# Token-block sums of a two-layer kernel: smaller column-tiled matmuls in place of a fold step, and a planner that expects later loads

## The chip, the cores and the metric

The kernel runs on one core of a Trainium2 chip. A core has a matrix engine (TensorE; PE in the profile, with its weight loads shown as PEld), a vector engine (VectorE, DVE), a scalar engine (ScalarE, ACT), a general engine (GpSimd, POOL), and a synchronising engine (SyncE, SP) that here only issues transfers. They share an on-chip memory of 128 partitions (SBUF) and an accumulator memory (PSUM) of eight banks, which TensorE writes. The metric is the device time of one execution in microseconds, as the median of several runs.

## The reference

The inputs are q, k, v of shape 8 x 8 x 576 x 64 (batch, head, token, dimension), a gain `g_norm` of 64, weights `w_in` (512 x 1024) and `w_out` (1024 x 512), and a gain `g_ln` of 1024.

```python
kv  = einsum('bhsd,bhse->bhde', k, v)          # 64 x 64 per head
out = einsum('bhsd,bhde->bhse', q, kv)
x   = out / sqrt(mean(out*out, -1) + 1e-6) * g_norm     # per head, then heads side by side: 4608 x 512
h   = x @ w_in
e   = exp(h - max(h));  solu = h * e / (sum(e) + 1e-9)  # along the 1024
ln  = (solu - mean(solu)) / sqrt(var(solu) + 1e-6) * g_ln
y   = ln @ w_out                                # 4608 x 512, float32
```

## The kernel before

The 4608 tokens are cut into nine chunks of 512: chunk c below 8 holds the first 512 tokens of batch c, and chunk 8 holds the last 64 tokens of all eight batches. The work of a chunk runs through these stages, each a planned piece with a name:

- Loads on GpSimd's queue bring k, v and q of a batch in bfloat16 (`load_kv`, `load_q`, L219 and L228). Batches 0 and 1 are loaded in two halves of four heads, later ones whole. `q_last` (L236) brings the last 64 tokens of a batch for chunk 8.
- `kv_mm` (L286) makes the 64 x 64 products of four head pairs with 64*64 tiles of TensorE; `kv_copy` (L305) copies them to SBUF.
- q is turned so that the head dimension lies along partitions: for chunks 0 to 3 with TensorE (`qT_mm`, L319, and a copy, L327), for chunks 4 to 8 (`XBAR`, L124) with a transposing transfer on SyncE's queue (`q_turn`, L336).
- `o_mm` (L343) multiplies by kv. A square (`sq`), a matmul with a table of means (`s_mm`, L373), a logarithm and an exponential on ScalarE (`ln`, `ex`) and a product on VectorE (`x_mul`, L392) give x, in four quarters (hf, z) per chunk.
- `h_mm` (L471) makes h transposed, 128 of the 1024 features at a time, in eight pieces of four 128x512 matmuls. ScalarE takes the exponential e (L482), VectorE the product u = h*e (L489), GpSimd or ScalarE the square of u (L500, L498), and GpSimd adds e of two pieces (L506).
- The statistics of the last layer are sums over 1024 features for each token: of u, of u*u and of e. `sums` (L531) forms them with TensorE. Its weight `stat_sel` is 32 columns wide, and column i holds 1/1024, so that the sum lands in row i of a quarter of 32 partitions. There are 8 + 8 + 4 = 20 matmuls of 128x512. Matmul n goes to quarter n % 4, so that four work at once, and each quarter ends with a part of each sum. `sums_turn` (L543) transposes 32 x 32 blocks on VectorE from PSUM to SBUF (128x512). `stats_mm` (L549) is the fold step: four float32 matmuls with `fold`, four identity matrices one above another, add up the four parts and put token r of a 128-token block on partition r. `stats` (L559) combines them in four short VectorE operations, and `rstd` (L570) takes the inverse root on ScalarE.
- `out_mm` (L591) multiplies u by the centred `w_out` in halves of four matmuls, two halves for each block of 128 tokens (m = 0 to 3). `scale` (L600) multiplies by rstd into `ob_sb`, and `store` (L607) sends it off on SyncE's queue.

The order of instructions on every engine is fixed before the run by a list scheduler, `Plan.order` (L33). It holds a clock for each engine. It repeatedly takes, among pieces whose needs are planned, the one that can start earliest by its clock, and of equals the one of the lowest rank (L47, L57). A piece can start when its engine is free, when its needs are done, and when the buffers that it claims (`first`) were let go by all their users (`uses`). The length given in `plan.add` is the time that it is believed to take. Loads pass through one shared queue (L75 to L78):

```python
            if load:
                queue = max(queue, t + length + 1.0) + load
                done[n] = queue + 1.3
```

A SyncE transpose counts as done 2.5 after its length (L74). At run time only real semaphores hold an engine up, but each engine executes in the planned order, so whatever waits holds up all behind it. Buffers that matter here: PSUM tags h, out and o have two banks each, s and misc one each. For chunk 0 the sums use a bank of h, for others misc. GpSimd issues the loads, and its own squares and additions stand in the same order.

Of the kernel before, what the change touches and what calls it, by code (L numbers as in the profile page):

```python
# [8 lines left out]
FP32 = mybir.dt.float32  # L9
# [3 lines left out]
MUL = mybir.AluOpType.mult  # L13
SUB = mybir.AluOpType.subtract
AF = mybir.ActivationFunctionType
PSUM = bass.MemoryType.PSUM


class Plan:
# [13 lines left out]
    def order(self):  # L33
        free, done, queue, lanes, mode = {}, {}, 2.5, [], {}
        held = {tag: [] for tag in self.bufs}
        waiting = {n: set(p[4]) for n, p in self.pieces.items()}
        behind = {}
        for n, needs in waiting.items():
            for m in needs:
                behind.setdefault(m, []).append(n)  # L40
        ready = [n for n, needs in waiting.items() if not needs]
        order = []
        while ready:
            best = None
            for n in ready:
                engine, length, rank, fn, needs, first, load = self.pieces[n]
                t = max([free.get(engine, 0.0)] + [done[m] for m in needs])  # L47
                more = {}
                for key in first:
                    old = held[key[0]] + more.setdefault(key[0], [])  # L50
                    more[key[0]].append(key)
                    if len(old) >= self.bufs[key[0]]:
                        last = self.users[old[-self.bufs[key[0]]]]
                        t = max([t] + [done.get(m, 1e9) for m in last])
                if load and len(lanes) >= 8:
                    t = max(t, lanes[-8])
                if t < 1e8 and (best is None or (t, rank) < best[:2]):  # L57
                    best = (t, rank, n)
            t, rank, n = best
            engine, length, rank, fn, needs, first, load = self.pieces[n]  # L60
            ready.remove(n)
            for key in first:
                held[key[0]].append(key)
            if engine == "pe":

                tiling = n[0] if n[0] in ("kv_mm", "o_mm", "sums", "st_mm") else "full"
                length += 0.1 if mode.get(engine, tiling) != tiling else 0.0
                mode[engine] = tiling
            if n[0] == "qT" and engine == "sp":

                if queue > t + 1.0:
                    length, queue = 2.2 * length, queue + 2.0
            free[engine] = t + length
            done[n] = t + length + {"pe": 0.2, "sp": 2.5}.get(engine, 0.12)  # L74
            if load:  # L75
                queue = max(queue, t + length + 1.0) + load
                done[n] = queue + 1.3
                lanes.append(done[n])  # L78
            order.append(fn)
            for m in behind.get(n, ()):  # L80
                waiting[m].discard(n)
                if not waiting[m]:
                    ready.append(m)
        assert len(order) == len(self.pieces)
        return order
# [3 lines left out]
def kernel(  # L89
# [20 lines left out]
    nc = tc.nc  # L110
# [9 lines left out]
    big = ctx.enter_context(tc.tile_pool(name="big", bufs=1))  # L120
# [3 lines left out]
    XBAR = tuple(range(4, NC))  # L124
    bufs = {
        "k": 3, "v": 3, "q": 3, "qT": 3, "osq": 4, "lss": 2, "rst": 2, "oc": 2, "x": 2, "e": 4, "u": 2, "usq": 2, "es": 2,
        "sumT": 2, "ob": 4,
    }

    def bank(key, shape, dtype):  # L130
        return ps.tile(shape, dtype, name=key[0] + "_ps", tag=key[0], bufs=banks[key[0]])

    def tile_of(key, shape, dtype):
        return sb.tile(shape, dtype, name=key[0] + "_sb", tag=key[0], bufs=bufs[key[0]])

    COPIED = ((0, 0),)
    plan = Plan({**banks, **bufs})
    T = {}
# [15 lines left out]

    ident = big.tile([128, 128], BF16, name="ident")
    eye = big.tile([NF, NF], FP32, name="eye")
    fold = big.tile([128, 32], FP32, name="fold")
    zeros = big.tile([128, 512], BF16, name="zeros")
    nc.vector.memset(zeros, 0.0)
    eps_t = big.tile([128, 1], FP32, name="eps_t")  # L160
# [46 lines left out]
        make_identity(nc, ident)  # L207
        make_identity(nc, eye)

    def make_fold():  # L210

        for j in range(4):
            nc.vector.tensor_copy(fold[32 * j:32 * j + 32, :], ident[32 * j:32 * j + 32, 32 * j:32 * j + 32])

    plan.add("ident", "pool", 1.0, -1.95, make_ident)
    plan.add("fold", "dve", 1.0, 0.2, make_fold, ["ident"])


    def load_kv(name, src, b, hs):  # L219
# [310 lines left out]

    def sums(c, part):  # L531
        if part == 0:
            T["sum", c] = bank(("misc" if c else "h", "sum", c), [128, 512], FP32)
        i, src = ((1, T["u", c]), (0, T["usq", c]), (2, T["es", c]))[part]
        n_src = NF // 2 if part == 2 else NF
        for n in range(n_src):
            j = n % 4
            nc.tensor.matmul(  # L538
                T["sum", c][32 * j:32 * j + 32, :], stat_sel[:, i, :], src[:, n, :],
                start=(part == 0 and n < 4), stop=(part == 2), tile_position=(0, 32 * j), skip_group_check=True,  # L540
            )

    def sums_turn(c):  # L543


        t = T["sumT", c] = tile_of(("sumT", c), [128, 4, 4, 32], FP32)
        nc.vector.transpose(t.rearrange("p a b c -> p (a b c)"), T["sum", c][:, :])

    def stats_mm(c):  # L549
        t = T["st", c] = bank(("misc", "st", c), [128, 4, 3], FP32)  # L550
        for g in range(4):
            nc.tensor.matmul(
                t[32 * g:32 * g + 32, :, :], fold[:, :], T["sumT", c][:, :, g, 0:3],
                start=True, stop=True, tile_position=(0, 32 * g),
            )

    small = ctx.enter_context(tc.tile_pool(name="small", bufs=2))

    def stats(c):  # L559

        st = T["st", c]
        w = small.tile([128, 4, 3], FP32, name="w")
        nc.vector.tensor_tensor(out=w[:, :, 1:3], in0=st[:, :, 1:3], in1=factors[:, :, :], op=MUL)
        nc.vector.memset(w[:, :, 0:1], 1.0)
        terms = small.tile([128, 4, 3], FP32, name="terms")
        nc.vector.tensor_tensor(out=terms[:, :, :], in0=st[:, :, :], in1=w[:, :, :], op=MUL)
        T["vare", c] = small.tile([128, 4], FP32, name="vare")
        nc.vector.tensor_reduce(out=T["vare", c][:, :], in_=terms[:, :, :], op=ADD, axis=mybir.AxisListType.X)  # L568

# [50 lines left out]
    for c in range(NC):  # L620
        r, rs = (c + 1, c + 1) if c else (0.55, -0.5)
        parts = [[("u", c, f) for f in range(NF)], [("usq", c, f) for f in range(NF)], [("es", c, n) for n in range(NF // 2)]]
        plan.add(("sums", c), "pe", 1.2, rs + 0.1, lambda c=c: [sums(c, part) for part in range(3)], sum(parts, []),
                 uses=[("u", c), ("usq", c), ("es", c)], first=[("misc" if c else "h", "sum", c)])
        plan.add(("turn", c), "dve", 0.62, rs + 0.14, lambda c=c: sums_turn(c), [("sums", c)],
                 uses=[("misc" if c else "h", "sum", c)], first=[("sumT", c)])
        plan.add(("st_mm", c), "pe", 0.15, rs + 0.15, lambda c=c: stats_mm(c), ["fold", ("turn", c)],
                 uses=[("sumT", c)], first=[("misc", "st", c)])
        plan.add(("stats", c), "dve", 0.65, rs + 0.16, lambda c=c: stats(c), [("st_mm", c)], uses=[("misc", "st", c)])
        plan.add(("rstd", c), "act", 0.45, rs + 0.17, lambda c=c: rstd(c), [("stats", c)])  # L630
        for m in range(4):
            tag = "o" if c == NC - 1 and m > 1 else "out"
            for half in range(2):
                plan.add(("out", c, m, half), "pe", 0.87, r + (2 * m + half) / 8 + 0.01,
                         lambda c=c, m=m, half=half, tag=tag: out_mm(c, m, half, tag),
                         [("w_center", f) for f in range(4 * half, 4 * half + 4)]
                         + [("u", c, f) for f in range(4 * half, 4 * half + 4)] + ([("out", c, m, 0)] if half else []),
                         uses=[("u", c)] + ([(tag, c, m)] if half else []), first=[] if half else [(tag, c, m)])
            plan.add(("ob", c, m), "act" if c == NC - 1 and m % 2 else "dve", 0.67, r + (2 * m + 2) / 8, lambda c=c, m=m: scale(c, m),
                     [("out", c, m, 1), ("rstd", c)], uses=[(tag, c, m)], first=[("ob", c, m)])  # L640
            plan.add(("store", c, m), "act" if c == NC - 1 and m % 2 else "sp", 0.6, r + (2 * m + 3) / 8, lambda c=c, m=m: store(c, m),
                     [("ob", c, m)], uses=[("ob", c, m)])
# [33 lines left out]
```

The softmax here doesn't subtract the row's maximum and nothing guards it: scores larger than these inputs give would overflow.

## Time and profile before

| what | value |
|---|---|
| median of 13 runs | 198.69 us (197.44 to 204.26) |
| the profiled execution, its own time | 199.1 us |
| its span, first to last instruction | 197.3 us |
| TensorE busy | 183.2 us (93%), 1806 matmuls |
| ScalarE, GpSimd, VectorE busy | 140.4, 129.0, 125.9 us |
| sums, L538: matmuls, mean of one | 180, 379 to 384 ns |
| fold step, L552: matmul records, mean of one | 72, 189 ns |
| transposes of sums, L547 | 9, 710 to 716 ns |
| loads of k, v, q, whole, issue to landing (median) | 12.3, 12.4, 14.2 us |
| transposing transfers | 5, 4.3 to 4.5 us |

A matmul's duration includes its way through the array, and neighbours overlap: four 128x512 matmuls that start one after another take 0.86 us in the chain, not four times 379 ns. So costs on TensorE are read from the starts of neighbours. A group's line names the engine, the operation, output and inputs, shapes, the count, the busy time and the mean. In a timeline, what stands in brackets at the end is the idle time of the engine ahead of this piece and what ended it.

### The profile page before, as it was taken

The page shows a single profiled execution, that of the slowest core. Times are in us where ns is not written, and L with a number is a line of the kernel's source. Part 1 is how long each engine was busy: PE and PEld are TensorE (multiplying, and loading weights), DVE is VectorE, ACT ScalarE, POOL GpSimd, SP SyncE. Part 2 cuts the span into 40 slices and gives each one's busy share as a digit, 9 for nine tenths or more (in the row PEclk, how much of TensorE's full clock was granted, in tenths as well). Part 3 has the DMA queues.
Part 4 walks back from the last instruction along what each step waited for, and adds up shares of the span by engine and source line. Part 5 has one row for each costly group of instructions (what it writes and reads, how often), then busy time and mean ns, then how long its engine had stood idle before and what let it go on. Part 6 is the DMA issues. An engine that isn't in the chain of part 4 may idle for free.

```text
span 197.3 us, 4481 instructions
## 1 busy us (share of the span) xinstructions
PE 183.2 (93%) x1806; PEld 82.8 (42%) x1806; DVE 125.9 (64%) x244; ACT 140.4 (71%) x244; POOL 129.0 (65%) x137
## 2 busy tenths in 40 slices
PE   7887988769999989999999999999999999999990
PEld 2442455325445434334444443443454444344430
DVE  2455587464878596578666948767584667665350
ACT  2038887884977899888889697889789296546421
POOL 7971799600899877887898685579194828845200
PEclk9999999978999999999999999999999999999998
DMA  4999999999995999699699983353112011211206
GB/s 52 190 203 293 326 203 205 202 208 242 207 243 53 196 203 241 137 187 210 134 158 228 203 169 115 116 104 120 53 53 74 35 59 51 106 53 70 94 18 195
DMA packets 35892, 29.65 MB, mean 150 GB/s; under 512 B 11800, under 2 KB 30240, under 8 KB 35872
## 3 DMA queue, kind: packets, MB, share of 16 engines
q0 software_dynamic: 20112, 17.30, 53.9%
q1 hardware_dynamic: 15472, 11.54, 20.9%
q10 hardware_dynamic: 288, 0.52, 0.9%
q8 instruction: 14, 0.23, 0.5%
q14 instruction: 6, 0.05, 0.1%
HBM read 32.51 MB, written 9.44 MB: 213 GB/s over the span
## 4 chain that ended last, share of the span: by engine, by line
PE 74%; DMA 11%; POOL 5%; ACT 4%; DVE 3%; issue 1%; POOLq 0%
PE out_ps L595 29%; PE h_ps L474 26%; DMA q_sb<-in_q_dram 7%; PE misc_ps L538 5%; DMA v_sb<-in_v_dram 3%; PE o_ps L354 3%; PE s_ps L375 3%; PE o_ps L595 2%; PE misc_ps L297 2%; POOL usq_sb L500 2%; DVE u_sb L489 1%; POOL k_sb L223 1%; PE misc_ps L198 1%; POOL v_sb L223 1%; PE misc_ps L325 1%
## 5 line engine op out<-in xcount | busy, mean ns | idle before, releaser
L474 PE MATMUL h_ps<-x_sb,w_in_sb 128*128 128x512 bf16 x276 | 70.0, 379 | 1.3 <-DVE x_sb L396 1.1
L595 PE MATMUL out_ps<-w_out_sb,u_sb 128*128 128x512 bf16 x272 | 70.4, 387 | 0.8 <-DVE ob_sb L605 0.7
L500 POOL TENSOR_TENSOR usq_sb<-u_sb 128x512 bf16<-128x512 bf16 x51 | 53.0, 1044 | 24.2 <-DVE u_sb L489 24.1
L506 POOL TENSOR_TENSOR es_sb<-e_sb 128x512 bf16<-128x512 f32 x36 | 45.8, 1274 | 25.7 <-ACT e_sb L482 25.4
L489 DVE TENSOR_TENSOR u_sb<-h_ps,e_sb 128x512 bf16<-128x512 f32 x69 | 47.2, 687 | 23.6 <-ACT e_sb L482 23.1
L482 ACT ACTIVATE e_sb<-h_ps,zero_t 128x512 f32<-128x512 f32 x69 | 47.1, 684 | 11.9 <-PE h_ps L474 11.5
L474 PEld LDWEIGHTS <-w_in_sb 128*128 128x128 bf16 x288 | 27.0, 98 | 34.7 <-issue 4.3
L595 PEld LDWEIGHTS <-u_sb 128*128 128x128 bf16 x288 | 26.9, 99 | 34.6 <-issue 6.6
L605 DVE TENSOR_SCALAR ob_sb<-out_ps,rstd 128x512 f32<-128x512 f32 x33 | 24.6, 746 | 12.0 <-PE out_ps L595 6.5
L396 DVE SCALAR_TENSOR_TENSOR x_sb<-o_ps,g_rep,rst_sb 128x512 bf16<-128x512 f32 x32 | 23.9, 749 | 9.5 <-ACT rst_sb L383 9.4
L369 ACT ACTIVATE osq_sb<-o_ps,zero_t 128x512 bf16<-128x512 f32 x31 | 19.8, 683 | 11.0 <-PE o_ps L354 10.9
L383 ACT ACTIVATE rst_sb<-lss_sb,zero_t 128x512 f32<-128x512 f32 x32 | 23.2, 725 | 0.6
L379 ACT ACTIVATE lss_sb<-s_ps,eps_t 128x512 f32<-128x512 f32 x32 | 22.0, 687 | 0.3 <-PE s_ps L375 0.2
L498 ACT ACTIVATE usq_sb<-u_sb,zero_t 128x512 bf16<-128x512 bf16 x21 | 15.1, 720 | 8.1 <-DVE u_sb L489 7.9
L375 PE MATMUL s_ps<-osq_sb,head_mean 128*128 128x512 bf16 x34 | 13.1, 385 | 0.9 <-ACT osq_sb L369 0.8
L223 POOL DMA_DIRECT2D k_sb<-in_k_dram x10 | 7.9, 788 | 4.1 <-DMA w_in_sb<-in_moe_w_in_dram 2.6
L198 PE MATMUL s_ps<-zeros 128*128 128x512 bf16 x28 | 9.2, 449 | 1.4 <-DVE zero_t L163 1.2
L231 POOL DMA_DIRECT2D q_sb<-in_q_dram x10 | 8.6, 858 | 2.0 <-DMA w_in_sb<-in_moe_w_in_dram 1.6
L315 DVE CAST kvd<-misc_ps 64x128 bf16<-64x128 f32 (+1 forms) x24 | 6.9, 288 | 4.5 <-PE s_ps L297 2.3
L572 ACT ACTIVATE lv<-vare,zero_t 128x4 f32<-128x4 f32 x9 | 2.7, 300 | 9.5 <-DVE vare L568 9.5
L297 PEld LDWEIGHTS <-k_sb 64*64 64x64 bf16 x576 | 6.7, 107 | 4.9 <-issue 4.9
L354 PE MATMUL o_ps<-qT_sb,kvd 64*64 64x32 bf16 (+1 forms) x240 | 8.3, 256 | 0.2 <-ACT qT_sb L332 0.2
(83 smaller groups left out, 139.0 us busy)
## 6 DMA issues: line engine op xcount, KB each, us to landing
out_dram<-ob_sb SPq DMA_DIRECT2D x34, 256.0 KB, 3.4
k_sb<-in_k_dram POOLq DMA_DIRECT2D x6, 576.0 KB, 12.3
v_sb<-in_v_dram POOLq DMA_DIRECT2D x6, 576.0 KB, 12.4
q_sb<-in_q_dram POOLq DMA_DIRECT2D x6, 512.0 KB, 14.2
w_out_f<-in_moe_w_out_dram POOLq DMA_DIRECT2D x1, 2048.0 KB, 16.6
k_sb<-in_k_dram POOLq DMA_DIRECT2D x4, 288.0 KB, 11.6
v_sb<-in_v_dram POOLq DMA_DIRECT2D x4, 288.0 KB, 12.3
q_sb<-in_q_dram POOLq DMA_DIRECT2D x4, 256.0 KB, 12.1
```

Of the source, the lines that this page charges most:

```text
L369: nc.scalar.activation(out=t[:, :], in_=T[("o", *i)].rearrange("p a b c -> p (a b c)"), func=AF.Square, bias=zero_t[:, :])
L375: nc.tensor.matmul(t[:, :], head_mean[:, :], T["osq", i][:, :], start=True, stop=True)
L379: nc.scalar.activation(out=t[:, :], in_=T["s", i][:, :], func=AF.Ln, bias=eps_t[:, :])
L383: nc.scalar.activation(out=t.rearrange("p a b c -> p (a b c)"), in_=T["lss", i][:, :], func=AF.Exp, scale=-0.5, bias=zero_t[:, :])
L396: nc.vector.scalar_tensor_tensor(out=T["x", c][:, 2 * hf:2 * hf + 2, z], in0=T["o", c, hf, z][:, :, :, :], scalar=g_rep[:, :], in1=T["rst" ...
L474: nc.tensor.matmul(t[:, :], w_in_sb[:, dt, f * 128:(f + 1) * 128], T["x", c][:, dt].rearrange("p a b c -> p (a b c)"), start=(dt == 0), st ...
L482: nc.scalar.activation(out=T["e", c, f // 2][:, f % 2, :], in_=T["h", c, f][:, :], func=AF.Exp, bias=zero_t[:, :])
L489: nc.vector.tensor_tensor(out=T["u", c][:, f, :], in0=T["h", c, f][:, :], in1=T["e", c, f // 2][:, f % 2, :], op=MUL)
L500: nc.gpsimd.tensor_tensor(out=dst, in0=src, in1=src, op=MUL)
L506: nc.gpsimd.tensor_tensor(out=T["es", c][:, n, :], in0=e[:, 0, :], in1=e[:, 1, :], op=ADD)
L595: nc.tensor.matmul(T["acc", c, m][:, :], T["u", c][:, f, m * 128:(m + 1) * 128], w_out_sb[:, f, :], start=(f == 0), stop=(f == NF - 1),)
L605: nc.vector.tensor_scalar_mul(out=t[:, :], in0=T["acc", c, m][:, :], scalar1=T["rstd", c][:, m:m + 1])
```

## The change

Two things change. First, in `sums` each matmul of 512 columns becomes four of 128, one to each quarter of 32 partitions. Quarter j takes the tokens of which the place within a block of 128 lies in 32j to 32j + 31, from all four blocks, and adds all sources n itself. No parts are left to be added. The sums fill 128 columns of their bank, VectorE transposes 32 x 32 blocks into the next 128 columns of the same bank, and `stats` reads its three numbers there. The fold matmuls, the fold table and the buffer `sumT` are gone, and the bank of the sums is held until `stats` has read it. The planner's length for the transpose is 0.25 in place of 0.62.

Second, the planner adds `LATE` = 4.0 to the time at which it believes that something has landed: loads of batches 2 and later (k, v, q and `q_last`), and the SyncE transposes. Loads of batches 0 and 1 and of the weights are left as they were.

```diff
+LATE = 4.0
...
-                tiling = n[0] if n[0] in ("kv_mm", "o_mm", "sums", "st_mm") else "full"
+                tiling = n[0] if n[0] in ("kv_mm", "o_mm", "sums") else "full"
...
-            done[n] = t + length + {"pe": 0.2, "sp": 2.5}.get(engine, 0.12)
+            done[n] = t + length + {"pe": 0.2, "sp": 2.5}.get(engine, 0.12) + (LATE if n[0] == "qT" and engine == "sp" else 0.0)
             if load:
                 queue = max(queue, t + length + 1.0) + load
-                done[n] = queue + 1.3
+                done[n] = queue + 1.3 + (0.0 if n[1] in (0, 1) or n == "w_out" else LATE)
...
-            T["sum", c] = bank(("misc" if c else "h", "sum", c), [128, 512], FP32)
+            T["sum", c] = bank(("misc" if c else "h", "sum", c), [128, 2, 128], FP32)
...
         for n in range(n_src):
-            j = n % 4
-            nc.tensor.matmul(
-                T["sum", c][32 * j:32 * j + 32, :], stat_sel[:, i, :], src[:, n, :],
-                start=(part == 0 and n < 4), stop=(part == 2), tile_position=(0, 32 * j), skip_group_check=True,
-            )
+            for j in range(4):
+
+                cols = src[:, n, :].rearrange("p (m j r) -> p j m r", m=4, j=4)[:, j]
+                nc.tensor.matmul(
+                    T["sum", c][32 * j:32 * j + 32, 0, :], stat_sel[:, i, :], cols, start=(part == 0 and n == 0),
+                    stop=(part == 2 and n == n_src - 1), tile_position=(0, 32 * j), skip_group_check=True,
+                )
...
-        t = T["sumT", c] = tile_of(("sumT", c), [128, 4, 4, 32], FP32)
-        nc.vector.transpose(t.rearrange("p a b c -> p (a b c)"), T["sum", c][:, :])
-
-    def stats_mm(c):
-        t = T["st", c] = bank(("misc", "st", c), [128, 4, 3], FP32)
-        for g in range(4):
-            nc.tensor.matmul(
-                t[32 * g:32 * g + 32, :, :], fold[:, :], T["sumT", c][:, :, g, 0:3],
-                start=True, stop=True, tile_position=(0, 32 * g),
-            )
+        T["st", c] = T["sum", c][:, 1, :].rearrange("p (m i) -> p m i", m=4)
+        nc.vector.transpose(T["sum", c][:, 1, :], T["sum", c][:, 0, :])
...
-        plan.add(("turn", c), "dve", 0.62, rs + 0.14, lambda c=c: sums_turn(c), [("sums", c)],
-                 uses=[("misc" if c else "h", "sum", c)], first=[("sumT", c)])
-        plan.add(("st_mm", c), "pe", 0.15, rs + 0.15, lambda c=c: stats_mm(c), ["fold", ("turn", c)],
-                 uses=[("sumT", c)], first=[("misc", "st", c)])
-        plan.add(("stats", c), "dve", 0.65, rs + 0.16, lambda c=c: stats(c), [("st_mm", c)], uses=[("misc", "st", c)])
+        plan.add(("turn", c), "dve", 0.25, rs + 0.14, lambda c=c: sums_turn(c), [("sums", c)],
+                 uses=[("misc" if c else "h", "sum", c)])
+        plan.add(("stats", c), "dve", 0.65, rs + 0.16, lambda c=c: stats(c), [("turn", c)], uses=[("misc" if c else "h", "sum", c)])
```

More of the change, by code (lines that the diff above doesn't have):

```diff
@@ L126 @@
         "k": 3, "v": 3, "q": 3, "qT": 3, "osq": 4, "lss": 2, "rst": 2, "oc": 2, "x": 2, "e": 4, "u": 2, "usq": 2, "es": 2,
-        "sumT": 2, "ob": 4,
+        "ob": 4,
     }
@@ L156 @@
     eye = big.tile([NF, NF], FP32, name="eye")
-    fold = big.tile([128, 32], FP32, name="fold")
     zeros = big.tile([128, 512], BF16, name="zeros")
@@ L208, in make_ident @@
         make_identity(nc, eye)
-    def make_fold():
-        for j in range(4):
-            nc.vector.tensor_copy(fold[32 * j:32 * j + 32, :], ident[32 * j:32 * j + 32, 32 * j:32 * j + 32])
     plan.add("ident", "pool", 1.0, -1.95, make_ident)
-    plan.add("fold", "dve", 1.0, 0.2, make_fold, ["ident"])
     def load_kv(name, src, b, hs):
@@ L565, in stats @@
         terms = small.tile([128, 4, 3], FP32, name="terms")
-        nc.vector.tensor_tensor(out=terms[:, :, :], in0=st[:, :, :], in1=w[:, :, :], op=MUL)
+        nc.vector.tensor_tensor(out=terms[:, :, :], in0=st[:, :, 0:3], in1=w[:, :, :], op=MUL)
         T["vare", c] = small.tile([128, 4], FP32, name="vare")
```

## The prediction

> **What bounds the kernel now.** I read the busy shares first, then busy time by stretch, then TensorE's own timeline where the change touches it.
>
> ```profile
> PE 183.2 (93%) x1806; PEld 82.8 (42%) x1806; DVE 125.9 (64%) x244; ACT 140.4 (71%) x244; POOL 129.0 (65%) x137
> ...
> PEclk9999999978999999999999999999999999999998
> ```
> ```profile
> 1.20:42.00 40.80, 34.04 (x346) 16.70 (x347) 23.23 (x53) 24.71 (x41) 29.45 (x37) 1.00 1.21 215
> 42.00:72.00 30.00, 28.97 (x388) 13.44 (x386) 21.33 (x41) 23.55 (x45) 19.77 (x20) 0.94 1.13 191
> 72.00:192.20 120.20, 120.19 (x1077) 52.61 (x1075) 80.97 (x149) 91.02 (x159) 79.57 (x76) 1.00 0.53 117
> ```
>
> Columns: stretch, length, busy us of PE, PEld, DVE, ACT, POOL, granted clock, DMA, GB/s. From 72 us to the end of matmuls TensorE never rests: there each TensorE microsecond is one of the span. From 1.2 to 72 it rests 7.8 us, and once its clock falls. The last 5.1 us are the last scaling and store.
>
> One block-sum sequence inside the full stretch (PE timeline: start, us, line, what; chunk 4):
>
> ```profile
> 117.62 0.38 PE L375 MATMUL s_ps<-osq_sb,head_mean 128*128 128x512 bf16 x1
> 117.93 0.61 PE L538 MATMUL misc_ps<-u_sb,stat_sel 128*32 128x512 bf16 x8
> 118.37 0.60 PE L538 MATMUL misc_ps<-usq_sb,stat_sel 128*32 128x512 bf16 x8
> 118.80 0.39 PE L538 MATMUL misc_ps<-es_sb,stat_sel 128*32 128x512 bf16 x4
> 119.12 1.04 PE L595 MATMUL out_ps<-w_out_sb,u_sb 128*128 128x512 bf16 x4
> 120.09 0.25 PE L552 MATMUL misc_ps<-sumT_sb,fold 128*32 128x12 f32 x8
> 120.27 0.39 PE L474 MATMUL h_ps<-x_sb,w_in_sb 128*128 128x512 bf16 x1
> ```
>
> The fold matmuls take 120.09 to 120.27 = 0.18 us, and the four L595 matmuls ahead of them last 0.97 us (119.12 to 120.09) where such a half between full-array work takes 0.86 (chain view): 0.11 for changing tiling. The fold step costs 0.29 us of TensorE.
>
> The stretch where TensorE rests most (same view):
>
> ```profile
> 37.22 0.39 PE L538 MATMUL h_ps<-es_sb,stat_sel 128*32 128x512 bf16 x4
> 38.60 0.25 PE L552 MATMUL misc_ps<-sumT_sb,fold 128*32 128x12 f32 x8 [0.99 <-ACT rst_sb L383]
> 38.78 0.41 PE L354 MATMUL h_ps<-qT_sb,kvd 64*64 64x256 bf16 x8
> 39.98 0.38 PE L375 MATMUL s_ps<-osq_sb,head_mean 128*128 128x512 bf16 x1 [0.78 <-ACT osq_sb L369]
> 41.54 0.62 PE L325 MATMUL misc_ps<-ident,q_sb 128*128 128x128 bf16 x8 [1.18 <-DMA q_sb<-in_q_dram]
> 41.99 0.56 PE L375 MATMUL s_ps<-osq_sb,head_mean 128*128 128x512 bf16 x1
> 42.34 3.44 PE L595 MATMUL out_ps<-w_out_sb,u_sb 128*128 128x512 bf16 x8
> ```
>
> Three waits, 0.99 + 0.78 + 1.18 = 2.95 us: for the transposed sums of chunk 0, for a square, for chunk 2's q. Then eight matmuls take 3.44 us instead of 1.73: a clock fall costs 1.7.
>
> **What the Trainium skill says.** "TensorEngine Tiling (Array Packing)", Key Properties: changing the tiling mode drains TensorE; the 0.11 us above agrees. "TensorE: Matmul & The Clock Gate", What's actually happening: idleness over a window near 3.4 us halves the clock for a window; the 3.44 us at half pace agrees. The same page, Back-to-back issue gap, puts an issue floor near 25 ns under small matmuls; this trace goes below it for tiled ones:
>
> ```profile
> 62.82 0.67 PEld L297 LDWEIGHTS <-k_sb 64*64 64x64 bf16 x72 [0.42 <-issue]
> 68.19 0.16 PEld L552 LDWEIGHTS misc_ps<-sumT_sb,fold 128*32 128x32 f32 x8 [0.42 <-issue]
> ```
>
> 72 loads start within 0.67 - 0.107 = 0.56 us, 8 ns each; eight 128*32 loads, the changed sums' own tile shape, start within 0.16 - 0.108 = 0.05 us, 7 ns each. The trace decides. "VectorE: DVE Perf Modes", The three transpose paths, gives 311 ns for a 128x128 transpose of another type.
>
> **The change part by part, on TensorE from 46 us on (chunks 1 to 8).**
>
> Removed: the fold step, 8 x 0.29 = 2.3 us.
>
> Resized: the sums go from 20 matmuls of 512 columns to 80 of 128; the streamed columns stay. Today's 20 take (119.12 - 0.10 - 117.93) = 1.09 us, 54.6 ns each, four tiles abreast: 53.3 streaming (213/4, from 0.86 us per four full matmuls) and 1.3 over. With the same excess per matmul: 80 x (13.3 + 1.3) = 1.17, +0.08 a chunk. Low end 0 (the excess belongs to columns, not matmuls). High end: the slowest tiled pace here, chunk 8's L354, 64 in 1.06 us, 16.6 ns: 1.33, +0.24. The new reads come in four runs of 32 per matmul, and L354's were single strided elements, so I stay near the low end: 8 x 0.09 = +0.7 us (0 to 1.9).
>
> VectorE: the transpose falls from 128x512 (0.71 us) to 128x128 within PSUM. Between the 12-element operation (0.17) and the 512-element ones (0.71), 128 elements come to 0.30. That the target is PSUM is shown nowhere; 0.25 to 0.71 holds it. VectorE is 67% busy from 72 on, so the saved 0.4 us a chunk is worth nothing there. The fold table's four copies (0.9 us at the start) lie beside the first loads: nothing.
>
> Latency: rstd comes earlier. For chunk 1 the transpose ended at 67.44, the fold matmuls waited behind an L474 piece until 68.19, statistics ran 68.55 to 69.13, and TensorE then rested 0.74 at 71.61 (before an out piece that waited for the freed bank, L605) and 0.16 before. Statistics straight after a 0.3 us transpose end about 1.4 us earlier: I take 0.7 of this 0.9. Elsewhere from 72 on there is no rest to win. The sum's bank is now held until the statistics end instead of the transpose; the next user of misc is a kv or transpose piece microseconds later, so I cost it at nothing. For chunk 0 it is h: o_mm(1,1) now waits for statistics, not the transpose, computed next.
>
> **The planner.** I follow its rules (L33 to L85) with the lengths in its add lines, for order only, never for time. Today it expects q(2) at 40.90 (landed: 26.96 + 14.5 = 41.5), q(3) at 49.4 (51.3), v(4) at 55.2 (57.8), q(4) at 57.9 (61.2), so loads are 0.6 to 3.3 us later than it thinks and 4.0 covers all. Where does 4 us bind? The first transpose of chunk 2 stood at 40.90, exactly its landing: it moves past 44.9. That of chunk 3 stood at 50.8 and moves past 53.4. kv_mm(2) stood at 43.36 against 42.2 late: free. From chunk 4 on consumers have room: DMA-transposed q of chunks 4, 5, 6, 7, 8 was due at 64.4, 81.1, 97.9, 119.3, 135.4 and used at 77.5, 94.0, 112.2, 130.5, 146.2, all over 8 late. A SyncE transpose that is planned 4 us later can change places with a store; stores have four buffers.
>
> Walking 37 to 45 by those rules: statistics straight after the transpose, rstd ahead of the squares, ob(0,0) about 1.5 us earlier, both out banks freed, so TensorE gets four out halves of chunk 0 before kv_mm(2) where it had two, and q(2) goes behind them. In trace durations: sums end 37.7; transpose to 38.1; statistics 0.57 to 38.7; o_mm(1,1) at 38.6 (was 38.78); rstd 0.6 to 39.4; square to 40.1; ob to 40.25; then TensorE is full from 40.15. Rests: 0.9 + 1.1 = 2.0 against 2.95, so 1.0 us gained. Next late is x(1): its last s_mm now stands behind two out halves, x at 44.7 (was 44.81), covered by the other two halves and kv_mm(2). The clock: whether a window still looks idle depends on its phase; I count 1.0 of the 1.7.
>
> Sum against the profiled 199.1 (span 197.3, 1.8 around it): -2.3 + 0.7 - 0.7 - 1.0 - 1.0 = -4.3, 194.8. The median 198.69 is 0.4 below that execution; since the clock fall may be what differs between runs, I don't subtract it again. Some of the early gain may wait for GpSimd, whose chunk 1 squares run nearly without a rest from 49 to 63.4 and end just ahead of sums(1) at 64.95. I say 195.0.
>
> **Rivals.**
> Early gain eaten: TensorE, ahead at 46, waits for GpSimd's squares or for ScalarE (9.4 of 10 us busy from 70 to 80). Only 2.3 - 0.7 = 1.6 is left: 197.1 to 197.5. For it: 64.95 against 63.4. Against: those chains start earlier too.
>
> Slower by order: chunk 2's transposes move back 4 us, x(2) comes late, and the out halves that could have filled TensorE are spent. Place: 57 to 64, ahead of h_mm(2,0) at 63.98. Today the first copy ends at 43.7 and is used at 48.70: 5 us of room; beyond it each microsecond is lost. 5 us more than I expect (a 3.4 us net loss after the 1.6) gives 199 to 202. Against: the move itself is 3.7.
>
> Slower by pace: the skill's 25 ns per small matmul: 80 x 25 = 2.0, +0.9 a chunk, 8 x 0.9 - 2.3 = +5 on the median, 203.7. It decides above (1.09 + 0.29)/80 = 17 ns. Against: 7 and 8 ns above.
>
> **Chances.** Forecast 0.57 (own range 193.2 to 197.0), gain eaten 0.23, order 0.14, pace 0.06. A difference under 0.5% (1 us) can't be told from no change. Faster than 197.7: nearly all of the first, six tenths of the second: 0.69. Same: 0.13. Slower: 0.18. The range 193.2 to 199.3 leaves out the pace, the worse half of order and the tail of full clock and rest gains.
>
> **What would show it.** No L552 rows; L538 matmuls x720 with sequences near 1.2 us; DVE transpose near 0.3; no tiling change between sums and the next one; four out halves ahead of h_mm(1,0); no q wait near 41; clock 1.00 in slices 9 and 10. Wrong if sums exceed 1.38 us, or TensorE rests between 46 and 192.

## The result: 0.8% faster, under half of what was forecast

Before: 198.88 us (median of 48 runs on this chip). After: 197.26 us (median of 11; 195.57 to 198.4). The ratio is 0.9922, 95% interval 0.9892 to 0.9952. The gain is 1.6 us where I forecast 3.7; the direction and the range held, the size did not. Some executions of most kernels here lie over 1.5% above the fastest of the same kernel, before the change and after it: times are medians of all executions, and ratios, spans and counts leave those out.

Most comparisons below are of spans, from the first to the last instruction, since the time around the span was 1.8 us nearly always, but 2.2 to 3.0 in four of the twelve executions of after that were taken, the profiled one (197.27 with a span of 194.3) among them. By spans the gain is about 2.2: the median is 194.8 after, and 196.9 and 197.2 before on the two chips of the experiments. And executions of one kernel differ in one thing that matters here: whether TensorE's clock fell for a window near 42 us. Their mean granted clock tells which: 0.989 or less with the fall, 0.991 or more without.

The page of after, its busy line and its clock line:

```profile
PE 179.6 (92%) x2274; PEld 87.9 (45%) x2274; DVE 121.7 (63%) x240; ACT 141.6 (73%) x244; POOL 129.0 (66%) x137
...
PEclk9999999999999999999999999999999999999998
```

The busy time by stretch (length, then busy us of PE, PEld, DVE, ACT, POOL, granted clock, DMA, GB/s):

```profile
1.20:42.00 40.80, 34.50 (x395) 17.59 (x396) 22.50 (x49) 24.61 (x41) 29.40 (x37) 1.00 1.21 214
42.00:72.00 30.00, 28.08 (x455) 14.09 (x454) 22.26 (x43) 25.32 (x47) 21.05 (x21) 1.00 1.14 193
72.00:189.20 117.20, 116.69 (x1428) 56.19 (x1426) 76.65 (x146) 90.55 (x157) 78.35 (x76) 1.00 0.60 121
```

In these stretches, from 1.2 us to the end of the matmuls, TensorE's busy time fell from 183.20 (34.04 + 28.97 + 120.19) to 179.27, by 3.93. Its rests grew from 7.80 (191.0 less 183.20) to 8.73. The difference, 3.0, is the whole fall of the span (197.3 to 194.3). I had forecast 2.6 less work (1.6 for the sums, 1.0 for the clock); of the 3.9 here, 1.7 are the clock fall, which this execution of before has and this one of after has not. And the rests, which I had expected to lose 1.7, grew by 0.9.

The block sums of chunk 4 in after (PE timeline: start, us, line, what):

```profile
116.52 0.63 PE L536 MATMUL misc_ps<-u_sb,stat_sel 128*32 128x128 bf16 x32
116.97 0.62 PE L536 MATMUL misc_ps<-usq_sb,stat_sel 128*32 128x128 bf16 x32
117.42 0.40 PE L536 MATMUL misc_ps<-es_sb,stat_sel 128*32 128x128 bf16 x16
117.75 1.04 PE L584 MATMUL out_ps<-w_out_sb,u_sb 128*128 128x512 bf16 x4
118.62 1.03 PE L470 MATMUL h_ps<-x_sb,w_in_sb 128*128 128x512 bf16 x4
```

The 80 small matmuls take 117.75 - 0.10 - 116.52 = 1.13 us, 14.1 ns each with their own weight loads; before, 20 large ones took 1.09. From the first sum to the h piece behind the out half it is 2.10 us (116.52 to 118.62) and was 2.34 (117.93 to 120.27). So a chunk saves 0.24, and eight save 1.9.

Where TensorE rests in after (same view; idle time and what ended it in brackets):

```profile
39.19 0.41 PE L350 MATMUL h_ps<-qT_sb,kvd 64*64 64x256 bf16 x7 [0.64 <-DVE terms L555]
40.62 0.38 PE L371 MATMUL s_ps<-osq_sb,head_mean 128*128 128x512 bf16 x1 [1.02 <-ACT osq_sb L365]
40.84 1.89 PE L584 MATMUL out_ps<-w_out_sb,u_sb 128*128 128x512 bf16 x8
...
42.78 1.89 PE L584 MATMUL out_ps<-w_out_sb,u_sb 128*128 128x512 bf16 x8
...
47.91 1.02 PE L470 MATMUL h_ps<-x_sb,w_in_sb 128*128 128x512 bf16 x4 [0.25 <-DVE u_sb L485]
...
52.23 0.38 PE L371 MATMUL s_ps<-osq_sb,head_mean 128*128 128x512 bf16 x1 [0.46 <-ACT lss_sb L375]
...
62.69 0.41 PE L350 MATMUL o_ps<-qT_sb,kvd 64*64 64x256 bf16 x7 [0.66 <-DVE x_sb L392]
...
67.99 1.02 PE L470 MATMUL h_ps<-x_sb,w_in_sb 128*128 128x512 bf16 x4 [0.42 <-DVE u_sb L485]
...
113.05 0.41 PE L350 MATMUL o_ps<-qT_sb,kvd 64*64 64x256 bf16 x8 [0.51 <-DMA qT_sb<-q_sb]
```

| rests of TensorE, us | before | after |
|---|---|---|
| 37 to 42 | 0.99 + 0.78 + 1.18 = 2.95 | 0.64 + 1.02 = 1.66 |
| 47 to 68, in chunks 1 and 2 | none over 0.2 | 0.25 + 0.46 + 0.66 + 0.42 = 1.79 |
| 71, for a freed out bank | 0.74 | none |
| 113, for chunk 6's transposed q | none | 0.51 |
| sum | 3.69 | 3.96 |

The early rests went as I said, and the one at 71 too. But 2.3 us of new ones stand behind them, which I had not forecast. The other 0.7 of the 0.9 is the start of this one execution: the last quarters of chunk 0's x were written from 18.61 on where it had been 17.93, after a longer wait for a load of v. That differs between executions and is no effect of the change.

### The profile page after: what moved, and what is told of

Same layout as the page of the kernel before. It is cut to its first block, busy times and chain, and to the rows that moved or that the text cites. A ratio compares the mean times of both kernels' runs of the same rounds, so it can differ in the third digit from the quotient of the medians.

```text
span 194.3 us, 5424 instructions
## 1 busy us (share of the span) xinstructions
PE 179.6 (92%) x2274; PEld 87.9 (45%) x2274; DVE 121.7 (63%) x240; ACT 141.6 (73%) x244; POOL 129.0 (66%) x137
## 4 chain that ended last, share of the span: by engine, by line
PE 70%; DMA 12%; ACT 6%; DVE 5%; POOL 3%; issue 1%; POOLq 0%; ACTq 0%
PE out_ps L584 27%; PE h_ps L470 24%; DMA qT_sb<-q_sb 8%; PE misc_ps L536 4%; DMA v_sb<-in_v_dram 4%; PE s_ps L371 3%; PE o_ps L350 3%; DVE w_out_sb L575 3%; ACT e_sb L478 2%; PE o_ps L584 2%; POOL k_sb L219 1%; PE misc_ps L293 1%; PE misc_ps L200 1%; PE misc_ps L321 1%; ACT lss_sb L375 1%
## 5 line engine op out<-in xcount | busy, mean ns | idle before, releaser
L584 PE MATMUL out_ps<-w_out_sb,u_sb 128*128 128x512 bf16 x272 | 68.8, 379 | 0.5 <-DVE w_out_sb L575 0.4
L536 PEld LDWEIGHTS <-stat_sel 128*32 128x32 bf16 x720 | 10.1, 97 | 3.7 <-issue 3.7
L293 PE MATMUL misc_ps<-v_sb,k_sb 64*64 64x64 bf16 x360 | 7.6, 194 | 1.6 <-DMA v_sb<-in_v_dram 1.6
```

What stands on the lines that cost most here:

```text
L584: nc.tensor.matmul(T["acc", c, m][:, :], T["u", c][:, f, m * 128:(m + 1) * 128], w_out_sb[:, f, :], start=(f == 0), stop=(f == NF - 1),)
```

## The experiments

What is open after the traces: is the lasting gain the sums' arithmetic alone? What is the clock fall worth? What does LATE do by itself? And why did the early lead not last? Zero matmuls serve as a tool: they put work on TensorE in its rests near 40 us, with results that nothing uses, so that the clock stays up.

### 1. Sums alone, in the old order

```diff
+        if c:
+            for n in range(n_src):
+                for j in range(4):
+                    cols = src[:, n, :].rearrange("p (m j r) -> p j m r", m=4, j=4)[:, j]
+                    nc.tensor.matmul(
+                        T["sum", c][32 * j:32 * j + 32, 0:128], stat_sel[:, i, :], cols, start=(part == 0 and n == 0),
...
     def stats_mm(c):
+        if c:
+            return
```

Chunks 1 to 8 have the changed sums and transposes and no fold; chunk 0 is as before, and so are the planner's entries, so that every piece keeps its old place.

> Chunks 1 to 8 take the new sums, without a fold step; chunk 0 keeps the old sums and fold, and every piece keeps its place in the old order. Theory A (the measured gain of 1.6 us is TensorE's saved work and nothing else): 8 x (0.29 - 0.04) = 2.0 us less, ratio 0.990, about the same as the whole change. Theory B (the saved work is smaller than read, and order brought part of the 1.6): under 1 us less, ratio above 0.995. Both: the span falls by the same amount at the same clock.

Measured: 198.68 us, ratio 0.9987 (0.996 to 1.0014): next to nothing of the 1.9. In its trace each chunk saves 0.28 at the place of the fold step. Its profile shows two things against that. Its clock fell for two windows instead of one (6.83 us at half pace, from 40.18 us on; 3.41 before); but only 2 of its 18 executions have a mean clock as low as that, so this does not explain the median. And TensorE paused once inside chunk 6's kv products (weight loads, PEld timeline):

```profile
109.47 0.24 PEld L297 LDWEIGHTS <-k_sb 64*64 64x64 bf16 x20 [1.12 <-issue]
```

Nothing that the profile shows was waited for ("issue"), and the last transfer on the instruction queue (16 KB, begun at 107.06 us) was just over. The page of after counts 468 matmuls more than that of before, and 17 such transfers where before had 14. So a new theory: more instructions cost TensorE regular pauses in their supply. (It is argued from one pause in one execution.) Runs 7 and 8 test it.

### 2. LATE alone

```diff
+LATE = 4.0
...
+            done[n] = t + length + {"pe": 0.2, "sp": 2.5}.get(engine, 0.12) + (LATE if n[0] == "qT" and engine == "sp" else 0.0)
...
+                done[n] = queue + 1.3 + (0.0 if n[1] in (0, 1) or n == "w_out" else LATE)
```

> Old sums with fold, the planner with the late landing of 4.0. Theory A: the new order neither gives nor takes, 1.00 within 0.003. Theory C (late landing moves SyncE's transposes beside the loads, and the delays eat early gain): slower by 0.5 to 1.5 us, ratio 1.003 to 1.008, with transposes that take over 6 us from issue to landing. Theory D (late landing is what closes the rest near 41 us): faster by about 1 us, ratio 0.995.

Measured: 199.30 us, ratio 1.0021 (1.0000 to 1.0043): no gain, at most a small loss. The clock fell in 19 of its 21 executions, for two windows in seven of them (granted clock near 0.981). Its transposing transfers landed 4.7 to 8.8 us after their issue, where before has 4.3 to 6.0.

### 3. The whole change without LATE

```diff
-LATE = 4.0
+LATE = 0.0
```

> The changed kernel with the late landing set to 0. Theory A: as the whole change, ratio 0.992. Theory C: better than the whole change by 0.5 to 1.5 us, ratio 0.985 to 0.989. Theory D: worse than the whole change by 1 us, ratio 0.997.

Measured: 196.59 us, ratio 0.989 (0.986 to 0.9921), no fall in any of 5 executions, span 194.3. That is what the changed kernel has without a fall too (194.35). So at a full clock nothing shows LATE to be worth anything; runs 9 to 12 settle it.

### 4 and 5. Zero matmuls in the rests, old and changed kernel

```diff
-    lambda c=c: [sums(c, part) for part in range(3)]
+    lambda c=c: [sums(c, part) for part in range(3)] + [warm(4, "misc") for _ in range(c == 0)]
...
-    lambda c=c, hf=hf, tag=tag: o_mm(c, hf, tag)
+    lambda c=c, hf=hf, tag=tag: [o_mm(c, hf, tag)] + [warm(3, "s") for _ in range((c, hf) == (1, 1))]
...
-    lambda c=c, hf=hf, tag=qtag: qT_mm(c, hf, tag)
+    lambda c=c, hf=hf, tag=qtag: [warm(5, "misc") for _ in range((c, hf) == (2, 0))] + [qT_mm(c, hf, tag)]
```

In the changed kernel it is three behind the sums and four behind `o_mm`, and none before the transposes.

> The kernel before, with zero matmuls (4, 3 and 5) put where TensorE rests at 37.6, 39.2 and 40.4 us, so that its clock doesn't fall at 42 us. If the fall at that place belongs to nearly every execution of the kernel before: about 1.7 us less, ratio 0.991 to 0.993, and granted clock 0.995 or more in nearly all runs. If it depends on the phase of a window and comes in half of them: 0.8 us less, ratio 0.996. If another place takes it over: no change.

> The changed kernel with zero matmuls (3 and 4) in TensorE's rests at 38 and 39.7 us, so that its clock doesn't fall. Half of the changed kernel's executions ran at a granted clock under 0.99, and their spans are 1.3 us longer. Theory F (the clock is one of the missing terms): full clock in nearly all runs, 196.2 us, ratio 0.987, and 1.3 us below the filled kernel before (197.5), so that the change itself is worth 1.3 at full clock. Rival: the fall moves to another place or the fill delays x of chunk 1: 197.2, no better than the whole change.

Measured: the old kernel with fill 197.54 us, ratio 0.9954 (0.9926 to 0.9983); the changed one 195.65, ratio 0.9833 (0.98 to 0.9867). No execution of either has the fall. Spans: 195.65 and 193.85. Executions of before with a fall have 197.0 on this chip, so the fall costs the old kernel up to 197.0 - 195.65 = 1.35 us of span. Without fill the difference is smaller and less even: its 13 executions without a fall have spans from 195.3 to 197.6, median 196.1, so something else that was not found lengthens about half of them. With fill in both, so at one clock, the change is worth 1.8, about the size of the arithmetic (1.9).

### 6. Is ScalarE what holds chunk 2 back?

Chunk 2's x was ready 17.3 and 17.4 us after chunk 1's in the two filled kernels (x(1) to x(2): 44.57 to 61.84, and 44.43 to 61.82), though the changed one had done more out halves by then. ScalarE was busy nearly throughout. So the kv copies of batches 2 to 5, half of them ScalarE's, go to VectorE:

```diff
-        return "act" if b == 1 or (b > 1 and x) else "dve"
+        return "act" if b == 1 or (b > 5 and x) else "dve"
```

> The changed kernel with the kv copies of batches 2 to 5 all on VectorE; ScalarE loses 3 copies of 0.27 us in each of these chunks. Theory G (from x of chunk 1 to x of chunk 2 ScalarE's own work sets the time, so TensorE's early lead is lost there): the first h piece of chunk 2 comes 0.5 to 1 us earlier after x of chunk 1, and the kernel gains 0.5 to 1 us over the whole change, ratio 0.987 to 0.990. Rival (TensorE's own order or the loads set it): no gain, ratio 0.992, with the same distance between those two points.

Measured: 196.02 us, ratio 0.9856 (0.9823 to 0.9889), span 194.25 without a fall, against 194.35 of the changed kernel. ScalarE's busy time from 42 to 72 us fell from 25.3 to 22.0, and the way from x(1) to x(2) got no shorter (45.36 to 63.59, 18.2 us). TensorE's waits for u grew instead (0.7 to 1.7 us). So taking these copies off ScalarE gains nothing. But the edit loads VectorE, which makes u and x, in exchange (22.3 to 23.8 us in the same stretch), so it doesn't clear ScalarE.

### 7 and 8. Do more instructions cost pauses?

Run 1 with the zero matmuls of run 4 added, then the same with one of the three fills cut into many small ones, 54 instructions more (a matmul and its weight load each) for about the same time (`warm` takes the columns of a matmul as its third argument):

```diff
-    [warm(3, "s") for _ in range((c, hf) == (1, 1))]
+    [warm(30, "s", 8) for _ in range((c, hf) == (1, 1))]
```

> The new sums in chunks 1 to 8 in the old order, with the fills of the filled kernel before. Theory H (the new sums save 0.28 us in each chunk, but at dense places TensorE waits for its instructions, which took back 1.2 to 1.4 us in the unfilled run): 0.3 to 0.8 us below the filled kernel before, 196.7 to 197.2, ratio 0.990 to 0.992, with a rest of 0.5 us or more inside a kv piece that no engine's work ends. Rival (the pause was a chance event): the full 2.0 us, 195.5, ratio 0.984.

> As the run before it, but one of the fills is made of 30 small matmuls instead of 3 large ones, 54 instructions more on TensorE and the same time, so that everything behind stands elsewhere in the blocks in which instructions are fetched. Theory H: the pause moves, shrinks or goes, and the time changes by over 0.5 us against the run before it. Rival (the pause is due to data or to buffers): it stays at the same piece with the same length, and the time is the same within 0.3 us.

Measured: 196.86 (ratio 0.989, 0.9841 to 0.994) and 197.7 us (0.989, 0.9825 to 0.9955), with spans of 194.6 and 194.55. The padding costs nothing, and in the trace of run 7 no wait without a cause is longer than 0.2 us. So more instructions alone don't bring pauses. For run 1 itself this leaves the question open: the same sums gain 1.05 with fill (195.65 to 194.6), but only 0.15 there (197.0 to 196.85, executions with a fall), and the missing 0.9 is about the length of its pause. Only one of its executions was profiled, so whether the pause is regular in that layout isn't shown.

Nor do the sums alone gain their 1.9 with fill. Run 12, the old kernel with fill, has the same order of pieces, so the two traces can be laid side by side. Blocks of sums start at 63.52 (chunk 1) and 116.50 (chunk 4) in run 12, and at 63.47 and 116.49 in run 7: what chunks 1 to 3 save is gone again. Only from there on is it kept, 0.26 a chunk: chunk 8's sums start at 184.78 and 183.74. TensorE's timeline of run 12 and then of run 7 shows where it goes:

```profile
70.17 1.02 PE L595 MATMUL out_ps<-w_out_sb,u_sb 128*128 128x512 bf16 x4 [0.74 <-DVE ob_sb L605]
...
85.18 1.04 PE L474 MATMUL h_ps<-x_sb,w_in_sb 128*128 128x512 bf16 x4
86.05 0.38 PE L375 MATMUL s_ps<-osq_sb,head_mean 128*128 128x512 bf16 x1
```
```profile
67.09 0.38 PE L375 MATMUL s_ps<-osq_sb,head_mean 128*128 128x512 bf16 x1 [0.28 <-ACT lss_sb L379]
...
70.17 1.02 PE L610 MATMUL out_ps<-w_out_sb,u_sb 128*128 128x512 bf16 x4 [0.74 <-DVE ob_sb L620]
...
84.92 1.04 PE L474 MATMUL h_ps<-x_sb,w_in_sb 128*128 128x512 bf16 x4
86.01 0.38 PE L375 MATMUL s_ps<-osq_sb,head_mean 128*128 128x512 bf16 x1
```

Behind chunk 1's sums run 7 waits 0.28 for a logarithm, and the rest of 0.74 then ends at the same moment in both. Behind chunk 2's, of the 0.26 gained by 84.92 all but 0.04 is gone at 86.01: the square that this matmul reads is ScalarE's, begun at 85.29 in run 7 and at 85.30 in run 12, 0.7 us long. The profile shows hardly a rest there (84.92 + 1.04 is 85.96), because a matmul that it shows as 0.38 us long can be followed by the next after 0.22, so that most of so short a wait is covered. TensorE looked full in this stretch and was only just in time for ScalarE. The whole change with fill, in its own order, has spans 0.75 (run 5) and 0.45 (run 11) below run 7.

### 9 to 12. Old or new sums, with or without LATE, all with fill on one chip

> The changed kernel with LATE = 0 and three zero matmuls behind the sums of chunk 0 (their results are used by nothing). Theory: with the clock held, the whole gain is TensorE's arithmetic, and the order that LATE gives is worth nothing: span 193.8 +-0.3, the same as the changed kernel with LATE and fill on the same chip. Rival (LATE spends TensorE's lead on out halves and brings x(2) later, and so costs time): span 193.1 or less, at least 0.7 below the changed kernel with LATE and fill.

> The old sums with LATE = 4.0 and zero matmuls at the same kind of places (four behind the sums of chunk 0, three or four behind o_mm(1,1)). Theory: at full clock the same span as the old kernel with fill, 195.65 +-0.3: the slower time of LATE alone was its clock. Rival (LATE costs time by its order): 196.3 or more.

> The changed kernel with fill once more, now on the chip of its three neighbours. Theory: span 193.85 +-0.3, and 1.8 below the old kernel with fill. Rival (part of that 1.8 was a difference between chips): 1.2 or less below it.

> The old kernel with fill once more. Theory: 195.65 +-0.3 of span at full clock, in nearly all executions. Rival (as above): 195.1 or less, or the clock falls in most executions, so that fill doesn't hold it.

The edits are those of runs 2 to 5, put together, with three (run 9), eight (run 10), seven (run 11) and twelve (run 12) zero matmuls near 40 us. Median time and span, us (no fall in an execution that counts):

| | LATE 0 | LATE 4 |
|---|---|---|
| old sums | 197.60; 195.7 | 197.44; 195.65 |
| new sums | 195.69; 193.9 | 195.93; 194.15 |

Ratios to the kernel before on this chip: 0.9939 (0.9913 to 0.9966) and 0.9933 (0.9912 to 0.9953) in the upper row, 0.984 (0.9792 to 0.9888) and 0.9851 (0.9798 to 0.9903) in the lower. The new sums are worth 1.8 and 1.5 us of span; LATE is worth nothing with either (-0.05, +0.25; the spans of run 9 lie between 193.7 and 194.6, those of run 11 between 193.4 and 195.2, so that the 0.25 is within their spread).

LATE does move things. The old kernel with fill has one wait of TensorE for other work from 40 us on, the one at 70.17 above. Here are those of the changed one with fill (run 11; engine, what waited, for what: us, times, longest):

```profile
PE o_ps L350 <- DMA qT_sb<-q_sb: 1.2, 1, 1.2
PE h_ps L470 <- DVE u_sb L485: 0.7, 2, 0.4
PE o_ps L350 <- DVE x_sb L392: 0.7, 1, 0.7
PE s_ps L371 <- ACT lss_sb L375: 0.5, 1, 0.5
```

and those of the same without LATE (run 9):

```profile
PE o_ps L350 <- DMA qT_sb<-q_sb: 1.0, 1, 1.0
PE misc_ps L293 <- DMA v_sb<-in_v_dram: 0.9, 1, 0.9
PE out_ps L584 <- DVE ob_sb L594: 0.7, 1, 0.7
PE misc_ps L321 <- issue: 0.6, 1, 0.6
PE h_ps L470 <- DVE u_sb L485: 0.6, 1, 0.6
PE s_ps L371 <- ACT osq_sb L365: 0.3, 1, 0.3
```

The two lists sum to 3.1 and 4.1 us, and name different work. Without LATE TensorE meets the late v of batch 3 and the out bank, which the planner's clock did not foresee. With LATE it has no wait for a load of k, v or q, but waits for x(2), u and the logarithm. Chunk 2's x came 3.3 us earlier without LATE (0.7 of it is the late start of after's execution): the write on VectorE that completes it starts at 61.89 in after and at 58.59 in run 9, where it comes 12.6 us behind x(1) and not 17.4. And both end alike. A lead that one order wins is spent at the next piece that is late.

## Why the prediction was wrong in size

Right, by its own steps:

- The fold step and the sums. I took -2.3 + 0.7 = -1.6; the trace has eight times 0.24, -1.9, and the runs at one clock 1.5 to 1.8. The added cost per chunk was 0.04, not 0.09; a slip is in it, since 0.86 us for four matmuls is 215 ns each and not 213, which makes the excess 0.9 ns per matmul and the +0.08 a +0.05. The rival "slower by pace" needed over 17 ns per small matmul; it is 14.1. The 25 ns floor of the Trainium skill ("TensorE: Matmul & The Clock Gate", Back-to-back issue gap) doesn't hold for tiled matmuls here. Full-array ones of 8 columns stay above it: 30 take 0.96 us in run 8, 32 ns each.
- VectorE's transpose inside PSUM: 0.30 taken, 0.324 measured for float32, next to the 311 ns, for bf16 and into SBUF, of "VectorE: DVE Perf Modes", The three transpose paths.
- The order: four out halves before h_mm(1,0), chunk 2's transposes behind it (47.04 us), no wait for q near 41. "Rests: 0.9 + 1.1 = 2.0 against 2.95": 1.66 came. The rest of 0.74 at 71 went too. "Slower by order" didn't come: x(2) was 1 us earlier than before, and at one clock (runs 4 and 5) at the same time.

Wrong:

- "so 1.0 us gained" and "I take 0.7 of this 0.9", the two terms for rests. The rests that I named did go (1.29 + 0.74 = 2.03 us), and 2.30 us of others took their place. The failed step is "Next late is x(1)", with its cover worked out and nothing behind it: I asked only what is late next, one step on, and then let the gain stand to the end. Behind x(1) stand u of chunk 1, then the logarithm, then x(2), each with no slack once TensorE comes early. The prediction's own sign of being wrong, rests between 46 and 192, came. The rival "early gain eaten" had the right shape and time (197.1 to 197.5; 197.26 came), but not the cause: I put it on GpSimd's squares or ScalarE's load. GpSimd is cleared: the squares of chunk 1 ended at 60.9 us, 3.3 before their sums began at 64.22. ScalarE is not: relieving it at VectorE's cost (run 6) gained nothing, but two of the new waits end with its logarithm and with x, which it feeds, and run 7's savings end at its logarithm and its square. What sets the 17.4 us from x(1) to x(2) was not taken apart further; 12.6 in run 9 shows that the order has a part in it.
- "From 72 us to the end of matmuls TensorE never rests: there each TensorE microsecond is one of the span." Runs 7 and 12 show otherwise for the old order: of what the sums save, chunks 1 to 3 lose all by 116 us, and the gain is 1.05.
- "From chunk 4 on consumers have room ... all over 8 late". The SyncE transposes cost 0.51 us in after's profile, 0.33 in run 5's and 1.19 in run 11's, at chunk 6. I had worked out when they are issued and not how long they take once they stand beside loads. LATE alone is not the cause: run 9, without it, waits 0.95 for chunk 4's transposed q, and run 10, LATE with the old sums, has no such wait (longest landing 9.1 us). In after two transposes begin at 62.17 and 96.52, 1.3 and 0.6 us behind the first load of a batch (60.86 and 95.97), and take 7.0 and 7.5 us to issue; in before the loads begin about 2 us or more behind the transpose, and its issue takes 1.6 to 3.2. That the loads cause it is read from this handful of transfers and was not tested. Their time from issue to landing, from the views of the tile of transposed q, of before and then of after:

```profile
DMA to landing us min/median/max: 4.3/4.3/6.0
```
```profile
DMA to landing us min/median/max: 6.6/11.5/16.5
```

- "I count 1.0 of the 1.7" for the clock. The mechanism is right: in the profile of before the clock falls for one window of 3.41 us to half pace, and a window of that length is what "TensorE: Matmul & The Clock Gate", What's actually happening, describes. The page speaks of an idle window, though, and here TensorE was busy for 1.44 of the 3.40 us before the fall (38.70 to 42.10); the measurement decides. With zero matmuls in the rests it fell in none of 77 executions. The size is off. I took it as certain in each run before and more than half removed. It fell in 67 of 80 executions before (in 11 of them for two windows) and in 6 of 12 after, at 1.3 us of span in after (195.65 to 194.35) and 1.35 to 1.5 against the filled old kernel: 0.34 x 1.4 = 0.5, an estimate.

The sum by measured terms, in span: -1.9 for the sums, +0.3 for the rests, -0.5 for the clock: -2.1, and the medians of spans say about -2.2. The +0.3 is from one pair of profiles. LATE has no lasting worth in it; what remains is TensorE's arithmetic and a third of a clock fall. But the arithmetic lasts nearly in full (1.5 to 1.8 of 1.9) only in the order that the planner makes for the new pieces, with LATE or without; in the old order 1.05 of it does. Why that order keeps more was not taken apart.

Three zero matmuls behind the sums and four behind `o_mm` of chunk 1 take away the falls that remain: 195.65 and 195.93 us on two chips, ratios 0.9833 and 0.9851, the fastest kernel of this study together with the same one without LATE (195.69).

## What to carry to other kernels

Work or a rest taken from an engine lasts only if the next waits behind have slack, so walk the chain through, and not only to the next late piece. That the profile shows an engine full is not enough: it may be just in time for its inputs, as TensorE was in chunks 1 to 3 of run 7, and then what it saves comes back as waits. A clock that falls for a window is an event with a frequency: count in how many runs it happens before pricing its removal, and try a few idle-time matmuls first. A transfer's room is counted from its landing time beside the traffic that it will meet in its new place.

## What was not expected of the hardware

- 80 matmuls of 128x128 with 32-column weights, a weight load for each, run at 14.1 ns apiece when four neighbours use four column groups: 1.13 us, against 1.09 for 20 of four times the width. Cutting tiled matmuls four times finer cost 4%.
- A transposing transfer on SyncE took 4.3 to 6.0 us to land before, and up to 16.5 us in after, where it stood at another moment between loads (16.0 in run 9).
- Whether the clock falls is close to a matter of chance in this kernel: 67 of 80 executions of the same program. With three to twelve zero matmuls near 40 us (39 in run 8, 30 of them small) it fell in none of 77; in runs 3 and 6, changed kernels without them, in none of 11 either. The window ahead of a fall need not be empty: TensorE was busy in 42% of it in the profile of before.
- One pause of 1.0 us in TensorE's supply of instructions, right after a 16 KB transfer on the instruction queue, in one profile (run 1), and one of 0.6 in another (run 9). What brings them on was not settled; 54 more instructions (run 8) did not.
- A wait of TensorE of 0.2 us can all but hide in a profile that shows it busy: matmuls shown as 0.38 us long start 0.22 apart. In run 7 the way from one piece to the next took 1.09 us (84.92 to 86.01) where run 12 has 0.87, and the gap shown is 0.05.
